# Weighted sums with V: from pT as the weights to V as the weights on four column tiles, with 32x32 transposes on VectorE

## The chip, the cores and the metric

The kernel runs on one core of a Trainium2 chip. The metric is the device time of one execution in microseconds; the time before is the median of three runs. The profile is one execution taken by the hardware profiler; its times count from the first instruction of its span.

## The reference

Two branches share the input x (2048 x 512, bf16) and are mixed by a gate per row. Branch A is attention with a compressive memory: 32 heads of 16, four segments of 512 rows, each causal in itself, plus what a running memory M (16 x 16 for each head) of the earlier segments gives. Branch B is a gated feed-forward of width 1792.

```python
g = sigmoid((x * gate_w).sum(-1, keepdims=True))
out = g * A(x) + (1 - g) * B(x)

# A, for each head and each of 4 segments of L = 512 rows
p = softmax(qs @ ks.T * scale + causal_mask)
a_dot = p @ vs
a_mem = (phi(qs) @ M) / (phi(qs) @ z + 1e-6)
o = sig(beta) * a_mem + (1 - sig(beta)) * a_dot
M += phi(ks).T @ vs ; z += phi(ks).sum(0)
# A = concat(o) @ wo ;  phi(t) = t + 1 if t > 0 else exp(t)

# B
B = (gelu(x @ w_gate) * (x @ w_up)) @ w_down
```

## The kernel before, in words

Everything stays on the chip. x is held transposed (xT), and the weights are loaded once. The work falls into four segments (s = 0 to 3), each with four head groups of eight heads (c = 0 to 3), and each head group is worked off in five *visits of the logits*, A to E: 80 visits in all, numbered here from 1 (visit 32 is segment 1, group 2, B; visit 57 is segment 2, group 3, B).

A visit (`group_qk`, lines 514 to 545) computes logits for four heads at once: four matmuls in row tiles of 32, one for each head, into one PSUM tile `lg` of four banks, of which there is only one. ScalarE exponentiates it in one instruction of 128 x 2048 into a tile `pT` (bf16, five buffers), and GpSimd zeroes the triangle above the diagonal. Logits are laid out with keys on partitions and queries along the free dimension, so `pT` is the transposed softmax numerator. A and B are the even heads (p = 0), C serves both, D and E the odd heads (p = 1); each visit takes one or two blocks of 128 keys.

The sums of values with weights (`pv`, lines 547 to 555) use a 128x128 block of `pT` as the stationary operand and 17 columns of V (16 values and a column of ones) as the moving one: 1280 matmuls of 17 columns over the kernel, into `od`, with queries on partitions. `finish` (557 to 566) takes the reciprocal of the 17th column, multiplies it by the gate of the head (`og`), and scales into `o2`. For segments 1 to 3 the memory's share `tm` (`mem_num`, 497 to 510) is added to `o2`. Then a transposing DMA on SyncE's queue (`tr_o`, line 570) turns `o2` into `oT`, which the output projection `aT` (line 417) reads as weights; the last head group is transposed by TensorE instead.

Between the visits TensorE is filled with *units* of other work, out of named streams: K projections (`kT`, whose result VectorE copies to `ktb` and masks into `KT`, lines 297 to 305), Q (`qT`), V (`vT`), gate and up projections of branch B (`gT`, `uT`), its down projection (`dT`, 14 matmuls a unit), the output projection (`aT`), the memory update (`MT`, line 441, which reads `pk` = phi(K) transposed by DMA from `phk`, line 312), the denominators of the memory (`zd`, line 480). A unit ends in VectorE's emptying of its PSUM bank; these units share three banks (pool `gen`).

The order is computed when the program is built, by a planner inside the kernel. It keeps a time for TensorE (`t_pe`), one for ScalarE (`t_act`) and the work that VectorE has not yet done (`backlog`), with a price for each step (`passed(pe, dve)`). In each visit it issues the logits, then what is due (`later(n, f)` puts a step n visits ahead), then fills TensorE up to a goal. Among streams it takes the one with the smallest due time plus a penalty for VectorE's work while `backlog` is high:

```python
st = min(hs, key=lambda x: x.q[0][5] + WEIGH * x.q[0][1] / x.q[0][0] *
         (backlog[0] - 0.8))
```

What a visit cannot do without is forced by `need` before its logits, such as the K of its head group. Each engine then runs its own list strictly in that order, and so does SyncE with the DMAs that it issues (`oT`, `pk`, the stores of `osb`).

Of the kernel before, what the change touches and what calls it, by code (L numbers as in the profile page):

```python
# [13 lines left out]
P = 128  # L14
# [20 lines left out]
EXP_T = 1.88  # L35
PHI_T = 1.06
# [8 lines left out]
def kernel(  # L45
# [54 lines left out]
    phk = const([P, NC8, L], BF, "phk")  # L100
# [5 lines left out]
    V = [const([P, KT, H, 18], BF, f"V{i}") for i in range(2)]  # L106
# [59 lines left out]
    def setup_consts():  # L166
        nc.gpsimd.memset(bm[:, :, :], 1.0)
        nc.gpsimd.affine_select(out=bm[:, :, :], in_=bm[:, :, :], pattern=[[-16, 8], [0, 17]],
                                compare_op=ALU.is_ge, fill=0.0, base=0, channel_multiplier=1)
        nc.gpsimd.affine_select(out=bm[:, :, :], in_=bm[:, :, :], pattern=[[16, 8], [0, 17]],  # L170
                                compare_op=ALU.is_ge, fill=0.0, base=15, channel_multiplier=-1)
        nc.vector.tensor_reduce(out=eo[:, 0:1], in_=bm[:, 0:8:2, 16],
                                axis=mybir.AxisListType.X, op=ALU.add)
        nc.vector.tensor_reduce(out=eo[:, 1:2], in_=bm[:, 1:8:2, 16],
                                axis=mybir.AxisListType.X, op=ALU.add)
        for i in range(2):
            nc.gpsimd.memset(V[i][:, :, :, 16:17], 1.0)
        nc.gpsimd.memset(Macc[:, :, :, :], 0.0)
# [8 lines left out]


# [76 lines left out]
    def phi(dst, src, key, lag):  # L265
        e = wk2.tile([P, 2, L], BF, name="phe", tag="phe")
        a = wk2.tile([P, 2, L], BF, name="pha", tag="pha", bufs=1)

        def f_exp():
            nc.scalar.activation(e[:, :, :], src, AF.Exp)  # L270
            act(PHI_T)

        def f_min():
            nc.vector.tensor_scalar(out=a[:, :, :], in0=src, scalar1=0.0, scalar2=1.0,  # L274
                                    op0=ALU.max, op1=ALU.add)
            nc.vector.tensor_tensor(out=dst, in0=e[:, :, :], in1=a[:, :, :], op=ALU.min)
            passed(0.0, 1.1)
            ready.add(key)

        later(lag, f_exp)  # L280
        later(lag + 1, f_min)
# [6 lines left out]
    def u_phk(s, c):  # L288
        def f():
            phi(phk[:, c:c + 2, :], ktb[:, c:c + 2, :], ("k", s, c), 1)  # L290
        return 0.0, 0.0, f
# [17 lines left out]
    def u_pk(s, c):  # L309
        def f():  # L310
            assert ("k", s, c - c % 2) in ready
            nc.sync.dma_start_transpose(pk[:, :, c * P:(c + 1) * P], phk[:, c, :])
        return 0.0, 0.0, f

    def u_v(s, kt):
        def f():
            T = gen("vT")
            for fc in range(FC):
                nc.tensor.matmul(T[:, :], lhsT=xT[:, fc, s * L + kt * P:s * L + (kt + 1) * P],  # L319
                                 rhs=wv[:, fc, :], start=(fc == 0), stop=(fc == FC - 1))  # L320
                if fc < FC - 1:
                    yield MM512
            nc.vector.tensor_copy(V[s % 2][:, kt, :, 0:16],
                                  T[:, :].rearrange("p (h d) -> p h d", h=H))
            return MM512
        return 4 * MM512, EVAC, f
# [107 lines left out]
    def u_M(s, half):  # L434
        def f():
            T = gen("MT")
            Tv = T[:, 0:272].rearrange("p (c h e) -> p c h e", c=2, h=8)
            for cc in range(2):
                c = 2 * half + cc
                for kt in range(KT):  # L440
                    nc.tensor.matmul(Tv[:, cc], lhsT=pk[:, kt, c * P:(c + 1) * P],  # L441
                                     rhs=V[s % 2][:, kt, 8 * c:8 * c + 8, 0:17],
# [54 lines left out]
    def mem_num(s, c):  # L497
# [12 lines left out]
        tms[c] = tm  # L510


# [34 lines left out]
    def pv(s, c, p, qqs, od, blocks):  # L547
        for qq in qqs:
            for j in range(4):
                for kt in range(qq + 1):  # L550
                    t, off = blocks[(p, kt)]
                    o = off + (qq - kt) * P
                    nc.tensor.matmul(od[:, qq, j, 0:17], lhsT=t[:, j, o:o + P],  # L553
                                     rhs=V[s % 2][:, kt, 8 * c + 2 * j + p, 0:17],
                                     start=(kt == 0), stop=(kt == qq))

    def finish(c, p, od, o2):
        rden = wk2.tile([P, KT, 4, 1], F32, name="rden", tag="rden")
        nc.vector.reciprocal(rden[:, :, :, :], od[:, :, :, 16:17])  # L559
        nc.vector.tensor_tensor(  # L560
            out=rden[:, :, :, 0], in0=rden[:, :, :, 0],
            in1=og[:, None, 8 * c + p:8 * c + 8:2].to_broadcast((P, KT, 4)), op=ALU.mult)
        nc.vector.tensor_tensor(  # L563
            out=o2[:, :, p, :], in0=od[:, :, :, 0:16].rearrange("p q j d -> p (q j) d"),
            in1=rden[:, :, :, :].rearrange("p q j o -> p (q j) o").to_broadcast((P, KT * 4, DH)),
            op=ALU.mult)

    def tr_o(c, o2, oT, by_dma):
        if by_dma:
            nc.sync.dma_start_transpose(  # L570
                oT[:, c, :].rearrange("p (q t) -> p q t", q=KT),
                o2[:, :, :, :].rearrange("p q r d -> p (q r d)"))
            return
        T = pgen.tile([P, 1024], BF, name="oTp", tag="gen")
        for qq in range(KT):
            nc.tensor.transpose(T[:, qq * P:(qq + 1) * P],
                                o2[:, 4 * qq:4 * qq + 4, :, :].rearrange("p j r d -> p (j r d)"),
                                ident[:, :])
        nc.vector.tensor_copy(oT[:, c, :], T[:, 0:512])


# [128 lines left out]
    for i in range(NK, NSEG * NC8):  # L710
# [3 lines left out]
                       (s == 0 or ("k", s - 1, c - c % 2) in ready)))  # L714
# [70 lines left out]
    def after(s, c, g, blk, oT, st):  # L785
        if g == "A":
            st["o2"] = wk2.tile([P, KT * 4, 2, DH], BF, name="o2", tag="o2")
        if g in "AD":
            st["od"] = pod.tile([P, KT, 4, 32], F32, name="od", tag="od")
        od, o2 = st["od"], st["o2"]  # L790
        p, qqs = {"A": (0, [0]), "B": (0, [1]), "C": (0, [2, 3]), "D": (1, [0]),
                  "E": (1, [1, 2, 3])}[g]
        pv(s, c, p, qqs, od, blk)
        passed(0.1 * sum(q + 1 for q in qqs))
        if g in "CE":
            finish(c, p, od, o2)
            passed(0.0, 0.85)
        if g == "B" and s > 0:
            room_for_bank()
            mem_num(s, c)  # L800
            passed(0.3, EVAC)
        if g == "E":
            if s > 0:
                nc.vector.tensor_tensor(
                    out=o2[:, :, :, :].rearrange("p q r d -> p (q r d)"),
                    in0=o2[:, :, :, :].rearrange("p q r d -> p (q r d)"),
                    in1=tms[c][:, :, :, :].rearrange("p q h d -> p (q h d)"), op=ALU.add)
                passed(0.0, 0.43)

            def tr():  # L810
                last = s == NSEG - 1 and c == NC8 - 1
                if last:
                    room_for_bank()
                tr_o(c, o2, oT, not last)
                done["tr", s] = count(("tr", s)) + 1
            later(2, tr)

    pending = []
    state = {}
    act_left[0] = 4 * NC8 * 5 * EXP_T + 3 * (GELU_T + 4 * PHI_T)  # L820
    for s in range(NSEG):
        oT = wk2.tile([P, FC, L], BF, name="oT", tag="oT")
        oTs[s] = oT
        for c in range(NC8):
            for g in "ABCDE":
                clock[0] += 1
                if g == "A":
                    need(("k", s), c + 1)
                    need(("q", s), c + 1)
                    need(("v", s), KT)  # L830
                t = group_qk(s, c, g)
                passed(QK_T)
                if g == "A":
                    mine = {(0, 0): (t, 0)}
# [13 lines left out]
                ready_at = t_act[0]  # L848
                for f in due.pop(clock[0], []):
                    f()  # L850
                n = 4 * NC8 * 5 - clock[0]
                pe_left = left() - TAIL_FILL - KT * 4 * MM512 + n * (QK_T + 0.55)
# [10 lines left out]
                pending.append(lambda a=(s, c, g, mine, oT, state): after(*a))  # L863
    fill_to(t_pe[0] + TAIL_FILL * 0.55)
    for f in pending:
# [13 lines left out]
    def phi_now(dst, src):  # L879
        e = wk2.tile([P, 2, L], BF, name="phe", tag="phe")  # L880
        a = wk2.tile([P, 2, L], BF, name="pha", tag="pha", bufs=1)
        nc.scalar.activation(e[:, :, :], src, AF.Exp)
        nc.vector.tensor_scalar(out=a[:, :, :], in0=src, scalar1=0.0, scalar2=1.0,
                                op0=ALU.max, op1=ALU.add)
        nc.vector.tensor_tensor(out=dst, in0=e[:, :, :], in1=a[:, :, :], op=ALU.min)
# [33 lines left out]
    def general():  # L919
# [3 lines left out]
        for s in range(NSEG):  # L923
# [17 lines left out]
            for c in range(NC8):  # L941
                o2 = wk2.tile([P, KT * 4, 2, DH], BF, name="o2", tag="o2")
                if s > 0:
                    mem_num(s, c)
                for p in range(2):
# [5 lines left out]
                    od = pod.tile([P, KT, 4, 32], F32, name="od", tag="od")  # L951
                    pv(s, c, p, range(KT), od, tiles)
                    finish(c, p, od, o2)
                if s > 0:
                    nc.vector.tensor_tensor(
                        out=o2[:, :, :, :].rearrange("p q r d -> p (q r d)"),
                        in0=o2[:, :, :, :].rearrange("p q r d -> p (q r d)"),
                        in1=tms[c][:, :, :, :].rearrange("p q h d -> p (q h d)"), op=ALU.add)
                tr_o(c, o2, oT, True)
# [9 lines left out]
            if s < NSEG - 1:  # L969
                for c in range(0, NC8, 2):  # L970
                    phi_now(phk[:, c:c + 2, :], ktb[:, c:c + 2, :])
# [39 lines left out]
```

## Time and profile before

| | us |
|---|---|
| median of the runs (3) | 291.42 (291.14 to 291.95) |
| span of the profiled execution | 289.4 |
| around the span, against the median | 2.0 |
| TensorE busy | 277.4 |
| VectorE busy | 215.5 |
| ScalarE busy | 200.7 |
| GpSimd busy | 82.7 |
| logits from the first to the last | 28.7 to 272.6 |

The profiled execution's own time is not listed apart from its span; it is taken as the span plus what lies between it and the median. In a row of the groups stand line, engine, operation, output and input, shapes and count; behind the bar the busy time, the mean duration in ns, and the idle time of the engine ahead of it with what ended most of it. A row of the timeline gives the start, the duration, and in brackets the idle time ahead. Durations include a part that overlaps the next instruction: matmuls of 512 columns last 0.38 and follow each other every 0.216.

### The profile page before, as it was taken

The numbers are of one execution on the slowest core, as the hardware profiler recorded it, in microseconds if no ns is written. First come the engines' busy times: TensorE is split into PE (matmuls) and PEld (weight loads), VectorE is DVE, ScalarE is ACT, GpSimd is POOL, SyncE is SP. The second block draws the span as 40 slices with busy tenths as digits, with TensorE's granted clock in tenths as the row PEclk, the third lists the DMA queues.
The fourth block names the chain that finished last, engine by engine and source line by source line (L and its number), as shares of the span: only waits on it lengthen the run. The fifth ranks groups of instructions, "written<-read, shape, count | busy, mean of one in ns | idle before, by whom it ended". The sixth has DMA issues, their size and how long they took to land.

```text
span 289.4 us, 6869 instructions
## 1 busy us (share of the span) xinstructions
PE 277.4 (96%) x2915; PEld 137.7 (48%) x2965; DVE 215.5 (74%) x422; ACT 200.7 (69%) x125; POOL 82.7 (29%) x140
## 2 busy tenths in 40 slices
PE   7999999999999999999999999999999999999994
PEld 3444454555444454555445444445454544444451
DVE  1897589768777869977878968988768567775545
ACT  3246977678898776776898785767658968677700
POOL 4000224334204424333410424242423033342410
PEclk9999999999999999999999999999999999999999
DMA  7989941110000100410000001032101001000102
GB/s 221 325 223 229 328 58 20 36 20 2 20 0 2 20 20 18 94 20 20 18 20 18 2 2 36 3 75 36 39 0 39 2 0 20 18 20 22 39 18 77
DMA packets 29441, 15.82 MB, mean 55 GB/s; under 512 B 21984, under 2 KB 28384, under 8 KB 29408
## 3 DMA queue, kind: packets, MB, share of 16 engines
q1 hardware_dynamic: 29408, 15.35, 21.1%
q8 instruction: 24, 0.39, 0.6%
q14 instruction: 9, 0.07, 0.1%
HBM read 8.14 MB, written 2.10 MB: 35 GB/s over the span
## 4 chain that ended last, share of the span: by engine, by line
PE 56%; DVE 3%; issue 1%; DVEq 0%
PE dT L400 14%; PE uT L384 10%; PE od L553 7%; PE gT L363 6%; PE lg L526 6%; PE aT L417 4%; PE kT L297 2%; PE vT L319 2%; PE qT L242 2%; PE mn L503 1%; PE MT L441 1%; DVE ktb L302 0%; DVE G L371 0%; DVE pha L274 0%; DVE o L563 0%
## 5 line engine op out<-in xcount | busy, mean ns | idle before, releaser
L532 ACT ACTIVATE pT<-lg 128x2048 bf16<-128x2048 f32 x80 | 150.1, 1876 | 57.0 <-PE lg L526 45.7
L543 POOL TENSOR_SCALAR_AFFINE_SELECT pT<-pT 128x512 bf16<-128x512 bf16 x128 | 79.5, 639 | 192.7 <-ACT pT L532 192.7
L384 PE MATMUL uT<-xT,wup 128*128 128x512 bf16 x208 | 59.5, 379 | 1.3 <-issue 0.6
L363 PE MATMUL gT<-xT,wga 128*128 128x512 bf16 x211 | 57.0, 379 | 1.0 <-DVE G L371 0.4
L400 PE MATMUL dT<-wdn,G 128*128 128x512 bf16 x212 | 53.2, 379 | 1.1 <-issue 0.3
L553 PEld LDWEIGHTS <-pT 128*128 128x128 bf16 x1280 | 43.6, 96 | 17.7 <-issue 0.4
L553 PE MATMUL od<-V,pT 128*128 128x17 bf16 x1280 | 43.9, 170 | 0.1
L390 DVE TENSOR_TENSOR G<-uT,G 128x512 bf16<-128x512 f32 x56 | 38.3, 685 | 7.2 <-PE uT L384 6.8
L371 DVE CAST G<-gT 128x512 bf16<-128x512 f32 x42 | 28.8, 685 | 8.0 <-PE gT L363 7.7
L526 PE MATMUL lg<-QT,KT 32*128 32x384 bf16 (+3 forms) x512 | 31.7, 301 | 1.6 <-issue 1.5
L363 PEld LDWEIGHTS <-wga 128*128 128x128 bf16 x224 | 19.7, 97 | 22.8 <-issue 5.5
L400 PEld LDWEIGHTS <-G 128*128 128x128 bf16 x224 | 19.5, 97 | 22.2 <-issue 3.9
L384 PEld LDWEIGHTS <-wup 128*128 128x128 bf16 x224 | 19.2, 97 | 20.8 <-issue 5.0
L405 DVE TENSOR_SCALAR tB<-dT,omg 128x512 bf16<-128x512 f32 x16 | 12.0, 750 | 19.9 <-PE dT L400 19.8
L526 PEld LDWEIGHTS <-KT 32*128 32x128 bf16 x512 | 8.9, 92 | 29.9 <-issue 29.5
L378 ACT ACTIVATE G<-G 128x3584 bf16<-128x3584 bf16 x6 | 18.8, 3182 | 0.0
L559 DVE RECIPROCAL rden<-od 128x16 f32<-128x16 f32 x32 | 8.2, 256 | 13.4 <-PE od L553 13.2
L297 PE MATMUL kT<-xT,wk 128*128 128x512 bf16 x63 | 16.8, 380 | 0.3 <-DVE xT L162 0.2
L417 PE MATMUL aT<-wo,oT 128*128 128x512 bf16 x63 | 16.4, 379 | 0.5 <-DVE G L371 0.5
L242 PE MATMUL qT<-xT,wq 128*128 128x512 bf16 x57 | 16.2, 379 | 0.5 <-DVE QT L247 0.2
L319 PE MATMUL vT<-wv,xT 128*128 128x512 bf16 x64 | 16.4, 380 | 0.0
L369 ACT ACTIVATE G<-gT 128x512 bf16<-128x512 f32 x14 | 8.4, 597 | 9.5 <-PE gT L363 9.5
(84 smaller groups left out, 224.7 us busy)
## 6 DMA issues: line engine op xcount, KB each, us to landing
wga<-in_B_w_gate_dram SPq DMA_DIRECT2D x1, 1792.0 KB, 12.6
wup<-in_B_w_up_dram SPq DMA_DIRECT2D x1, 1792.0 KB, 9.1
wdn<-in_B_w_down_dram SPq DMA_DIRECT2D x1, 1792.0 KB, 9.1
out_dram<-osb SPq DMA_DIRECT2D x12, 128.0 KB, 1.7
G<-in_A_x_dram SPq DMA_DIRECT2D x1, 512.0 KB, 4.1
wk<-in_A_wk_dram SPq DMA_DIRECT2D x1, 512.0 KB, 5.0
wq<-in_A_wq_dram SPq DMA_DIRECT2D x1, 512.0 KB, 6.7
wv<-in_A_wv_dram SPq DMA_DIRECT2D x1, 512.0 KB, 8.7
```

Of the source, the lines that this page charges most:

```text
L297: nc.tensor.matmul(T[:, :], lhsT=wk[:, fc, c * P:(c + 1) * P], rhs=xT[:, fc, s * L:(s + 1) * L], start=(fc == 0), stop=(fc == FC - 1))
L319: nc.tensor.matmul(T[:, :], lhsT=xT[:, fc, s * L + kt * P:s * L + (kt + 1) * P], rhs=wv[:, fc, :], start=(fc == 0), stop=(fc == FC - 1))
L363: nc.tensor.matmul(T[:, :], lhsT=wga[:, fc, hs * P:(hs + 1) * P], rhs=xT[:, fc, s * L:(s + 1) * L], start=(fc == 0), stop=(fc == FC - 1))
L371: nc.vector.tensor_copy(G[s % NG][:, hs, :], T[:, :])
L384: nc.tensor.matmul(T[:, :], lhsT=wup[:, fc, hs * P:(hs + 1) * P], rhs=xT[:, fc, s * L:(s + 1) * L], start=(fc == 0), stop=(fc == FC - 1))
L390: nc.vector.tensor_tensor(out=g, in0=T[:, :], in1=g, op=ALU.mult)
L400: nc.tensor.matmul(T[:, :], lhsT=G[s % NG][:, hs, qt * P:(qt + 1) * P], rhs=wdn[:, hs, :], start=(hs == 0), stop=(hs == HS - 1))
L417: nc.tensor.matmul(T[:, :], lhsT=oT[:, fc, qt * P:(qt + 1) * P], rhs=wo[:, fc, :], start=(fc == 0), stop=(fc == FC - 1))
L526: nc.tensor.matmul(lg[:, j, off:off + n], lhsT=KTm[pp][32 * j:32 * j + 32, (NC8 * s + c) % NK, kt * P:(kt + 1) * P], rhs=QT[32 * j:32 * j ...
L532: nc.scalar.activation(pT[:, :, :], lg[:, :, :], AF.Exp, scale=DH ** -0.5)
L543: nc.gpsimd.affine_select(out=v, in_=v, pattern=pat, compare_op=ALU.is_ge, fill=0.0, base=0, channel_multiplier=-1)
L553: nc.tensor.matmul(od[:, qq, j, 0:17], lhsT=t[:, j, o:o + P], rhs=V[s % 2][:, kt, 8 * c + 2 * j + p, 0:17], start=(kt == 0), stop=(kt == qq))
```

## The change

V becomes the stationary operand. For one parity of a head group, once all its blocks of `pT` are there, a *lump* of 16 matmuls runs directly behind the logits of a visit: for each of four key blocks and each of four heads, 32 columns of V (16 values, ones, and what follows) are the weights on one of four column tiles, and up to 512 columns of `pT` stream. The lump of the even heads stands in visit E, that of the odd heads in B of the next head group. The result `od` has values on partitions and queries along the free dimension. VectorE transposes it in 32x32 blocks out of PSUM into `oq` (fp32), one visit later takes the reciprocal and scales into `o2` (`norm`), and two visits after the second lump transposes 32x32 blocks back into `oT` (`back`). The memory's share `tm` is now transposed by a DMA on SyncE's queue into `mT` as soon as it is computed, and added at `oT` (`add_mem`), three visits after the second lump; the DMAs of `oT` and the transposes on TensorE are gone.

Beside that: phi is computed in place (no `pha`, no `phk`), so `pk` is transposed from `ktb`, and a K unit may start only when the `pk` transpose of its head group in the segment before has been issued; V gets 16 more columns of ones at its end; the numerator (`mem_num`) is issued in visit B from a list of its own; the planner's prices change (`PV_T = 0.65` for a lump, 0.69 for the transpose, 0.7 for `norm`, 0.6 for `back`).

```diff
-    def pv(s, c, p, qqs, od, blocks):
-        for qq in qqs:
+    def pv(s, c, p, blocks):
+        od = pod.tile([P, L], F32, name="od", tag="od")
+        for kt in range(KT):
+            t, off = blocks[(p, kt)]
+            n = L - kt * P
             for j in range(4):
-                for kt in range(qq + 1):
-                    t, off = blocks[(p, kt)]
-                    o = off + (qq - kt) * P
-                    nc.tensor.matmul(od[:, qq, j, 0:17], lhsT=t[:, j, o:o + P],
-                                     rhs=V[s % 2][:, kt, 8 * c + 2 * j + p, 0:17],
-                                     start=(kt == 0), stop=(kt == qq))
-    def finish(c, p, od, o2):
...
+                h = 8 * c + 2 * j + p
+                nc.tensor.matmul(od[32 * j:32 * j + 32, kt * P:L],
+                                 lhsT=V[s % 2][:, kt, 18 * h:18 * h + 32],
+                                 rhs=t[:, j, off:off + n],
+                                 start=(kt == 0), stop=(kt == KT - 1),
+                                 tile_position=(0, 32 * j))
+        oq = wk2.tile([P, 16, 32], F32, name="oq", tag="oq")
+        nc.vector.transpose(oq[:, :, :].rearrange("p b r -> p (b r)"), od[:, :])
+        return oq
+    def norm(c, p, oq, o2):
+        rden = wk2.tile([P, 16, 1], F32, name="rden", tag="rden")
+        nc.vector.reciprocal(rden[:, :, :], oq[:, :, 16:17])
+        nc.vector.scalar_tensor_tensor(
+            out=o2[:, :, p, :], in0=oq[:, :, 0:16], scalar=ogs[:, c, p:p + 1],
+            in1=rden[:, :, :].to_broadcast((P, 16, DH)), op0=ALU.mult, op1=ALU.mult)
+    def back(c, o2, oT):
+        nc.vector.transpose(oT[:, c, :], o2[:, :, :, :].rearrange("p b r d -> p (b r d)"))
+    def add_mem(c, oT):
+        nc.vector.tensor_tensor(out=oT[:, c, :], in0=oT[:, c, :], in1=tms[c][:, :], op=ALU.add)
     def mem_num(s, c):
...
-        tms[c] = tm
+        mT = wk2.tile([P, L], BF, name="mT", tag="mT")
+        nc.sync.dma_start_transpose(mT[:, :].rearrange("p (q t) -> p q t", q=KT),
+                                    tm[:, :, :, :].rearrange("p q h d -> p (q h d)"))
+        tms[c] = mT
     def u_phk(s, c):
-            phi(phk[:, c:c + 2, :], ktb[:, c:c + 2, :], ("k", s, c), 1)
+            phi(ktb[:, c:c + 2, :], ktb[:, c:c + 2, :], ("k", s, c), 1)
     def u_pk(s, c):
-            nc.sync.dma_start_transpose(pk[:, :, c * P:(c + 1) * P], phk[:, c, :])
+            nc.sync.dma_start_transpose(pk[:, :, c * P:(c + 1) * P], ktb[:, c, :])
...
-                       (s == 0 or ("k", s - 1, c - c % 2) in ready)))
+                       (s == 0 or count(("pk", s - 1)) > c)))
+    def lump(s, c, p, st, oT):
...
+        oq = pv(s, c, p, st["blk"])
+        passed(PV_T, EVAC)
...
+        later(1, f_norm)
+        if p == 1:
+            later(2, f_back)
+            if s > 0:
+                later(3, f_add)
...
+                if g == "B":
+                    for f in waiting:
+                        f()
+                    waiting.clear()
+                if g == "E":
+                    lump(s, c, 0, state, oT)
+                    waiting.append(lambda a=(s, c, 1, state, oT): lump(*a))
...
+                if g == "A" and s > 0:
+                    pending.append(lambda a=(s, c): numerator(*a))
```

## The prediction

> **What bounds the kernel now.** I read the page's busy times and chain first, then the groups, then the timeline around single visits of the logits, then the issues of SyncE.
>
> ```profile
> PE 277.4 (96%) x2915; PEld 137.7 (48%) x2965; DVE 215.5 (74%) x422; ACT 200.7 (69%) x125; POOL 82.7 (29%) x140
> ...
> PE 56%; DVE 3%; issue 1%; DVEq 0%
> ...
> L532 ACT ACTIVATE pT<-lg 128x2048 bf16<-128x2048 f32 x80 | 150.1, 1876 | 57.0 <-PE lg L526 45.7
> ...
> L553 PE MATMUL od<-V,pT 128*128 128x17 bf16 x1280 | 43.9, 170 | 0.1
> ```
>
> TensorE (PE) is busy nearly all the time and holds the chain. The exps of ScalarE stand idle 57 us beside them, 45.7 of it waiting for logits. Is that slack large? The timeline of two visits that follow closely says no:
>
> ```profile
> 252.06 0.40 PE L526 MATMUL lg<-QT,KT 32*128 32x384 bf16 x8
> ...
> 252.39 0.76 PEld L400 LDWEIGHTS <-G 128*128 128x128 bf16 x5 [0.21 <-issue]
> ...
> 252.59 1.88 ACT L532 ACTIVATE pT<-lg 128x2048 bf16<-128x2048 f32 x1 [0.58 <-PE lg L526]
> ...
> 254.54 0.12 PEld L526 LDWEIGHTS <-KT 32*128 32x128 bf16 x8 [0.42 <-issue]
> ...
> 255.05 1.88 ACT L532 ACTIVATE pT<-lg 128x2048 bf16<-128x2048 f32 x1 [0.58 <-PE lg L526]
> ```
>
> There is one logits tile, so logits wait for the exp before and the exp for the logits. Where TensorE arrives early a visit still takes 1.876 + 0.58 = 2.456 us: a floor under every visit. Logits cost TensorE 0.33 (252.06 to 252.39) plus 0.10 by which the matmul ahead is stretched at the change of tile shape; that gives 0.43.
>
> I added up what the order of instructions puts between each logits and the next: 0.216 per 512-column matmul, 0.0247 per od matmul (36 stand for 0.89 in the chain), 0.43 per logits. Visits 1 to 79 before come to 240.0 us; the trace has 243.9 from the first logits (28.7) to the last (272.6). So TensorE streams nearly without holes, and 77 of the 79 visits lie above the floor.
>
> **The change, part by part.**
>
> *Removed on TensorE.* 1280 od matmuls x 0.0247 = 31.6 us, and four transposes at the end (0.2).
>
> *Added on TensorE.* 32 lumps of 16 matmuls in four column tiles. If the tiles run together a lump is (512+384+256+128) columns x 0.216/512 = 0.54, and it makes one more change of shape (0.11, the excess of the logits' 0.33 over their 512 columns): 0.65, or 20.8 us in all. Do they run together? The warm-up has this shape:
>
> ```profile
> 4.01 0.62 PE L151 MATMUL warm<-G 128*32 128x256 bf16 x8
> ```
>
> ```profile
> 4.01 0.14 PEld L151 LDWEIGHTS <-G 128*32 128x32 bf16 x8 [0.84 <-issue]
> ```
>
> Eight 256-column matmuls, each lasting 0.41 there, took 0.62 together; in series at that clock they would need 1.7. All loads were through by 4.15.
>
> *What of 31.6 - 20.8 = 10.8 us is kept.* In the order of the changed kernel visits 1 to 79 sum to 229.1, but 48 of them hold only some 2.37 us and are stopped by the floor. With 2.456 for those the sum is 233.4, so the gain is 240.1 - 233.4 = **-6.7 us**. A cheaper lump would hardly add to it.
>
> *VectorE.* Per pair of lumps it loses two finishes (reciprocal 0.26, two products 0.32 and 0.43) and gains two transposes of od, two reciprocals, two products, one transpose back. No row has a transpose. The nearest are 128x512 from PSUM at 0.685 (0.60 from start to start when queued) and 128x512 bf16 at 0.425 or, reduced, 0.677. I take 0.60 for both kinds, the PSUM row being nearest; ends 0.35 and 1.2, the latter if four-byte elements go at half rate. VectorE then works about 1.3 us more per head group, 21 us in all, and comes to some 0.85 of TensorE's time in most stretches instead of 0.72. On average that is hidden. It is not where TensorE waits for one particular result, in three kinds of place.
>
> *First: pk behind the new mT on SyncE.* oT transposes leave the queue, twelve mT transposes enter it, issued as soon as the numerator exists. Issue is in order, and each waits for its data:
>
> ```profile
> 116.43 0.36 SPq L430 DMA_DIRECT2D out_dram<-osb  x1
> 116.88 5.33 SPq L312 DMA_TRANSPOSE pk<-phk  x4
> ```
>
> ```profile
> DMA to landing us min/median/max: 2.5/2.7/4.9
> ```
>
> A transpose holds SyncE 1.2 to 1.3 us and lands 2.5 after its issue. Before, pk's first piece landed near 119.4 and MT read it at 122.5: 3 us to spare. In the new order the four pk issues of segment 1 stand behind an mT whose tm is produced in visit 32, and MT follows in visit 33. From the logits of visit 32: lump done 0.98, handed over 1.2; VectorE then has transpose 0.60, reduction 0.59, phi 0.51 + 0.61, G 0.60, the three rdm steps 0.98, tm 0.69: 5.8. mT occupies SyncE to 7.0, pk lands at 9.5 and 10.8, MT is through at 11.0. Without waits TensorE would be there at lump 0.98, uT 0.86, zd and mn 0.42, gT 0.43, logits 0.43, gT 0.43, MT 0.5: 4.1. **+6.9 us**, with the next logits behind it and so ScalarE.
>
> In segment 2 MT's second half is in visit 58, right behind the first, and its pk stands behind an osb store. From the logits of visit 57: VectorE 1.2, transpose, G, tm 1.8, phi 1.1, norm 0.6, osb 0.75: 5.5; store issue 5.9, pk lands at 8.4 and 9.7, MT through at 10.0 instead of 4.3. **+5.7 us**. Segment 0 has seven visits between the two and pays nothing. Bounds for the two: 0 each if VectorE is far ahead, 8 each with slow transposes or the longest landing (4.9).
>
> *Second: K in the last moment.* The planner prices VectorE's new work and pushes the K units, dear on VectorE, back until they are forced. In visits 40, 50, 55, 60 and 75 kT stands with 4, 0, 0, 4 and 2 matmuls between it and the logits that need it. From its last column to those logits: result 0.17, ktb 0.73, KT 0.40, two hand-overs 0.2: 1.5. Less what stands between (0.86, 0, 0, 0.86, 0.43): **+5.3 us**. Bounds 2 and 9. These visits hold 3.8 us or more, so the floor does not cover it. Before, kT stood at least a visit ahead.
>
> *Third: single banks.* Behind transposes VectorE empties the three general banks late; before, such waits were 0.3 to 0.6 apiece (TensorE idle 0.49 at 114.16). Some four more: **+2** (0 to 4).
>
> *Other edits.* phi in place: same instructions, 0. ktb is now read by the pk transposes before K may overwrite it; K comes six visits later or more, 0 (1 if late). Adding tm at oT instead of o2: same 0.43. The tail gets transpose, norms, back and add (some 3.2 us) against 13 dT matmuls (2.8): **+0.5**.
>
> *Clock.* The steps of the first loads (1.75, 2.17, 2.60, 3.03) are 0.43, twice 0.216, until 5.76; 3.4 us behind the last matmul the granted clock falls:
>
> ```profile
> 286.00:289.00 3.00, 0.00 (x0) 0.00 (x0) 0.37 (x2) 0.00 (x0) 0.00 (x0) 1.00 0.29 98
> 289.00:289.40 0.40, 0.00 (x0) 0.00 (x0) 0.00 (x0) 0.00 (x0) 0.00 (x0) 0.58 0.00 0
> ```
>
> The two pk waits leave TensorE idle for 4 to 5 us in a piece. If the clock falls there, some 4.4 us run at half speed as at the start, a loss of 2.2 each. I count one: **+2.2** (0 to 4.4). The Trainium skill (TensorE: Matmul & The Clock Gate, Part 1) says that the gate halves the clock after an idle window of about 3.4 us which runs free of the kernel. By that rule either idle may or may not contain a whole window, which gives the same 0 to 4.4; the trace's one fall agrees with the 3.4.
>
> **Sum** against the profiled execution: 289.4 - 6.7 + 6.9 + 5.7 + 5.3 + 2 + 0.5 + 2.2 = 305.3. Its span lies 2.0 under the median of 291.42, so 307.
>
> **Rivals.**
>
> *The waits don't bite (faster).* If pk has landed when MT comes and K's chain is hidden, only floor, banks and tail count: 291.4 - 6.7 + 2.5 = 287. For it: the average load of VectorE leaves 15%. Against it: the issue order, and durations that the trace has. It decides where the two pk waits and the K waits together fall under 4 us. 0.10, and 0.02 that the parts cancel to within 0.3% (what a measurement can tell here).
>
> *Slow transposes.* At 1.2 each od transpose adds 0.6 ahead of the two pk places and the five K places (4.2) and more bank waits (3): 314. No row excludes it. 0.14.
>
> *Loads that do not overlap.* If a round's four loads wait for the round before, 0.1 each round (a load of that shape lasts 0.106), a lump is 0.95: visits B and E rise from 2.36 to 2.66, 0.2 over the floor, 32 x 0.2 = 6.4: 313. The warm-up's loads speak against it: the second four were through before the second four matmuls began. 0.08. The Trainium skill (same page, Part 3) says that loads overlap running matmuls only where the row group differs, which column tiles share; the warm-up's rows disagree.
>
> *Column tiles in series.* A lump of 2.1: 32 x 1.5 more, over 345. Warm-up against it: 0.01.
>
> **Numbers.** The forecast's own case, 300 to 312: 0.57; waits at half size, 293 to 300: 0.08. Faster 0.10, same 0.02, slower 0.88. The range 296 to 318 leaves out the fast case and the extremes. The Trainium skill (VectorE: DVE Perf Modes, The three transpose paths) gives 311 ns for 128x128 bf16; by that an estimate for 512 columns is 0.71, and the sum 1 us more.
>
> **What would show it.** In the trace after: lumps of 0.65; logits at 2.46 us in most visits; TensorE idle 4 to 6 us before MT in visits 33 and 58, released by a DMA; 0.5 to 1.5 us before the logits of visits 41, 51, 56, 61, 76, released by KT; VectorE near 237 busy. I am wrong if MT waits under 2 us in both places, or if the transposes run far from 0.6.

## The result, and the profile after

The changed kernel takes 306.34 us (median, 305.73 to 306.76) against 291.28: ratio 1.0497 (1.0461 to 1.0534). The forecast was 307, slower.

First the page of the changed kernel: busy times, the granted clock in 40 slices, the shares of the chain, and two rows of the groups.

```profile
PE 279.7 (92%) x2193; PEld 118.5 (39%) x2193; DVE 236.3 (78%) x441; ACT 200.6 (66%) x125; POOL 84.2 (28%) x142
PEclk9999999999999999669999999999789999999999
PE 77%; DVE 14%; DMA 3%; issue 2%; ACT 2%; SPq 1%; DVEq 0%; ACTq 0%
L539 ACT ACTIVATE pT<-lg 128x2048 bf16<-128x2048 f32 x80 | 150.1, 1876 | 72.8 <-PE lg L533 67.4
L567 DVE STREAM_TRANSPOSE oq<-od 128x512 f32<-128x512 f32 x32 | 22.9, 715 | 16.8 <-PE od L561 16.4
```

TensorE has 772 matmuls fewer (by its weight loads, 2193 instead of 2965; the page of before lacks 50 matmul records) and yet 2.3 us more of busy time, in part because two stretches ran at half clock: warm_mt below, whose clock stays up, has 282.5 us, of which 36 added matmuls of 0.216 make 7.8, so 5.0 us less than here. VectorE's share of the chain went from 3% to 14%. The exps wait 72.8 us instead of 57.0.

TensorE's waits in the whole run (total, times, longest):

```profile
PE MT L447 <- DMA pk<-ktb: 10.4, 4, 5.0
PE lg L533 <- DVE KT L310: 4.2, 5, 1.2
PE gT L369 <- DVE G L396: 2.3, 1, 2.3
```

Where they lie is seen when the time between the logits of chosen visits is compared (starts in the timeline, us). Visits 32 and 33 lie in the column "30 to 35", visits 57 and 58 in "55 to 60":

| kernel | 1 to 30 | 30 to 35 | 35 to 55 | 55 to 60 | 60 to 80 |
|---|---|---|---|---|---|
| before | 88.80 | 13.32 | 64.06 | 13.54 | 64.14 |
| after | 84.40 | 22.99 | 66.06 | 23.28 | 62.80 |

So the changed kernel is ahead by 4.4 us at visit 30, loses 9.7 at each of the two places and 2.0 between them, and wins 1.3 behind them. With 0.3 won before the first logits and a tail as long as before that is 15.3 us, the difference of the two spans (304.7 against 289.4).

Place 1, SyncE's queue and then TensorE:

```profile
124.24 1.20 SPq L517 DMA_TRANSPOSE mT<-tm  x1
125.53 5.14 SPq L318 DMA_TRANSPOSE pk<-ktb  x4
```

```profile
122.49 0.59 PE L369 MATMUL gT<-xT,wga 128*128 128x512 bf16 x2 [2.35 <-DVE G L396]
...
128.00 0.63 PE L447 MATMUL MT<-V,pk 128*128 128x136 bf16 x4 [4.05 <-DMA pk<-ktb]
129.32 0.63 PE L447 MATMUL MT<-V,pk 128*128 128x136 bf16 x4 [0.69 <-DMA pk<-ktb]
```

mT, whose tm VectorE made until 124.2, stood ahead of all four pk transposes. The first two, which this MT reads, were held by nothing else: VectorE had finished their phi at 91.99. The phi of the other two was done at 121.84. MT was through (the next unit could start) 12.1 us after the logits of visit 32 (11.0 in the forecast). Place 2, the same two views:

```profile
215.50 0.34 SPq L436 DMA_DIRECT2D out_dram<-osb  x1
215.88 2.50 SPq L318 DMA_TRANSPOSE pk<-ktb  x2
```

```profile
218.34 0.64 PE L447 MATMUL MT<-V,pk 128*128 128x136 bf16 x4 [5.02 <-DMA pk<-ktb]
219.66 0.63 PE L447 MATMUL MT<-V,pk 128*128 128x136 bf16 x4 [0.69 <-DMA pk<-ktb]
```

Here it was 10.7 us (10.0 in the forecast). Elsewhere the floor is plain to see, in ScalarE's timeline near the end: exps of 1.88 with 0.5 to 0.6 between them, one every 2.4 us.

```profile
281.18 1.88 ACT L539 ACTIVATE pT<-lg 128x2048 bf16<-128x2048 f32 x1 [0.58 <-PE lg L533]
283.62 1.88 ACT L539 ACTIVATE pT<-lg 128x2048 bf16<-128x2048 f32 x1 [0.56 <-PE lg L533]
285.99 1.88 ACT L539 ACTIVATE pT<-lg 128x2048 bf16<-128x2048 f32 x1 [0.49 <-PE lg L533]
```

### The profile page after: what moved, and what is told of

It reads as the page before. It is cut to its first block, busy times and chain, and to the rows that moved or that the text cites. A ratio compares the mean times of both kernels' runs of the same rounds, so it can differ in the third digit from the quotient of the medians.

```text
span 304.7 us, 5365 instructions
## 1 busy us (share of the span) xinstructions
PE 279.7 (92%) x2193; PEld 118.5 (39%) x2193; DVE 236.3 (78%) x441; ACT 200.6 (66%) x125; POOL 84.2 (28%) x142
## 4 chain that ended last, share of the span: by engine, by line
PE 77%; DVE 14%; DMA 3%; issue 2%; ACT 2%; SPq 1%; DVEq 0%; ACTq 0%
PE dT L406 15%; PE uT L390 14%; PE gT L369 14%; PE lg L533 9%; PE od L561 7%; PE vT L325 4%; PE aT L423 4%; PE qT L249 4%; PE kT L303 4%; DVE ktb L308 2%; DVE KT L310 2%; DMA pk<-ktb 2%; DVE G L396 1%; DMA G<-in_A_x_dram 1%; ACT pT L539 1%
## 5 line engine op out<-in xcount | busy, mean ns | idle before, releaser
L539 ACT ACTIVATE pT<-lg 128x2048 bf16<-128x2048 f32 x80 | 150.1, 1876 | 72.8 <-PE lg L533 67.4
L550 POOL TENSOR_SCALAR_AFFINE_SELECT pT<-pT 128x512 bf16<-128x512 bf16 x128 | 81.4, 654 | 206.6 <-ACT pT L539 206.6
L369 PE MATMUL gT<-xT,wga 128*128 128x512 bf16 x224 | 59.3, 389 | 2.4 <-DVE G L396 2.3
L390 PE MATMUL uT<-xT,wup 128*128 128x512 bf16 x224 | 61.0, 385 | 0.5 <-DVE G L377 0.4
L567 DVE STREAM_TRANSPOSE oq<-od 128x512 f32<-128x512 f32 x32 | 22.9, 715 | 16.8 <-PE od L561 16.4
L406 PEld LDWEIGHTS <-G 128*128 128x128 bf16 x224 | 20.7, 98 | 25.3 <-issue 3.1
L533 PEld LDWEIGHTS <-KT 32*128 32x128 bf16 x512 | 11.0, 92 | 37.6 <-issue 30.5
L561 PE MATMUL od<-pT,V 128*32 128x256 bf16 (+3 forms) x512 | 23.3, 302 | 0.0
L249 PE MATMUL qT<-xT,wq 128*128 128x512 bf16 x64 | 17.4, 391 | 0.3 <-DVE QT L254 0.2
L573 DVE SCALAR_TENSOR_TENSOR o<-oq,ogs,rden 128x256 bf16<-128x256 f32 x32 | 16.6, 518 | 1.1
L561 PEld LDWEIGHTS <-V 128*32 128x32 bf16 x512 | 10.7, 96 | 12.2 <-issue 6.3
```

Of the source, the lines that this page charges most:

```text
L249: nc.tensor.matmul(T[:, :], lhsT=wq[:, fc, c * P:(c + 1) * P], rhs=xT[:, fc, s * L:(s + 1) * L], start=(fc == 0), stop=(fc == FC - 1))
L369: nc.tensor.matmul(T[:, :], lhsT=wga[:, fc, hs * P:(hs + 1) * P], rhs=xT[:, fc, s * L:(s + 1) * L], start=(fc == 0), stop=(fc == FC - 1))
L390: nc.tensor.matmul(T[:, :], lhsT=wup[:, fc, hs * P:(hs + 1) * P], rhs=xT[:, fc, s * L:(s + 1) * L], start=(fc == 0), stop=(fc == FC - 1))
L406: nc.tensor.matmul(T[:, :], lhsT=G[s % NG][:, hs, qt * P:(qt + 1) * P], rhs=wdn[:, hs, :], start=(hs == 0), stop=(hs == HS - 1))
L533: nc.tensor.matmul(lg[:, j, off:off + n], lhsT=KTm[pp][32 * j:32 * j + 32, (NC8 * s + c) % NK, kt * P:(kt + 1) * P], rhs=QT[32 * j:32 * j ...
L539: nc.scalar.activation(pT[:, :, :], lg[:, :, :], AF.Exp, scale=DH ** -0.5)
```

## The experiments

The theory: the loss is made of late results at named places (pk at two, K at five), of the half clock that the long waits bring, and of a floor that keeps most of TensorE's saving from being seen. The main rival: VectorE, with 21 us more work, is too full as such, and TensorE waits for whatever comes next. All edits are to the changed kernel unless said. Ratios are against the kernel before, which took 291.27 to 291.33 beside them. The five columns are read from the one profiled execution of each; those of late_m and short_lumps took 298.66 and 289.58 us, 1.3 and 2.1 over their medians, and each holds a window at half clock in the column "30 to 35".

| kernel | median us | ratio (95%) | 1 to 30 | 30 to 35 | 35 to 55 | 55 to 60 | 60 to 80 |
|---|---|---|---|---|---|---|---|
| warm_mt | 301.91 | 1.0374 (1.0355 to 1.0392) | 84.40 | 20.34 | 66.05 | 21.40 | 62.80 |
| queue_order | 297.58 | 1.0223 (1.0204 to 1.0241) | 84.40 | 16.03 | 66.05 | 20.99 | 62.79 |
| late_m | 297.40 | 1.0204 (1.0171 to 1.0237) | 84.40 | 16.99 | 66.66 | 16.79 | 67.61 |
| early_k | 296.32 | 1.0176 (1.0159 to 1.0193) | 84.40 | 22.39 | 65.43 | 15.12 | 62.05 |
| late_m_early_k | 290.96 | 0.9996 (0.9978 to 1.0014) | 84.40 | 15.59 | 65.39 | 15.51 | 63.64 |
| unpriced | 294.53 | 1.0097 (1.0068 to 1.0126) | 89.36 | 13.76 | 67.84 | 13.21 | 62.82 |
| transpose_twice | 320.51 | 1.1017 (1.0986 to 1.1048) | 88.38 | 23.53 | 69.79 | 23.39 | 66.13 |
| short_lumps | 287.51 | 0.9869 (0.9853 to 0.9886) | 83.76 | 17.04 | 64.82 | 15.51 | 62.15 |
| half_transposes | 287.54 | 0.9873 (0.9851 to 0.9896) | 84.14 | 14.69 | 65.04 | 15.51 | 61.58 |
| add_on_gpsimd | 294.83 | 1.0129 (1.0084 to 1.0174) | 84.39 | 17.24 | 65.15 | 16.41 | 64.22 |
| tuned | 288.02 | 0.9885 (0.9869 to 0.9902) | 85.39 | 14.40 | 63.68 | 15.30 | 62.77 |
| tuned_on_vector | 287.61 | 0.9871 (0.9852 to 0.9891) | 88.21 | 12.91 | 63.95 | 12.66 | 63.24 |

**warm_mt: the price of the clock alone.**

```diff
             T = gen("MT")
+            for i in range({(1, 0): 16, (2, 1): 20}.get((s, half), 0) * (not general_now[0])):
+                nc.tensor.matmul(T[:, :], lhsT=wq[:, 0, 0:P], rhs=xT[:, 0, 0:L],
+                                 start=True, stop=True)
```

> Ahead of the two MT units that wait for pk (segment 1 first half, segment 2 second half) 16 and 20 matmuls of 512 columns run into MT's own bank; the real matmuls overwrite them. They fill 3.5 and 4.3 us of the 4.05 and 5.02 us of idle time; the waits stay. It prices the clock alone. Theory: the granted clock stays full and the two drops cost what the forecast bounded, 2.2 each: 302 to 304. Rival (behind the waits the exps and VectorE set the pace, so a slow TensorE costs nothing): 306 within 1 us, though the clock stays full.

4.4 us came of it. At place 1 the added matmuls fill the idle time, and MT starts where it did (127.96 against 128.00):

```profile
123.76 3.62 PE L444 MATMUL MT<-xT,wq 128*128 128x512 bf16 x16
127.96 0.42 PE L450 MATMUL MT<-V,pk 128*128 128x136 bf16 x4 [0.58 <-DMA pk<-ktb]
```

Four MT matmuls take 0.42 instead of 0.63, and the clock row has no slice under 9. The half clock cost 2.65 us at place 1 (22.99 to 20.34) and 1.88 at place 2: the upper end of the forecast's bound for both together, not the one drop that it counted. The rival that a slow TensorE would cost nothing there is out.

**queue_order: mT and osb one visit later in SyncE's queue.**

```diff
-        nc.sync.dma_start_transpose(mT[:, :].rearrange("p (q t) -> p q t", q=KT),
-                                    tm[:, :, :, :].rearrange("p q h d -> p (q h d)"))
+        send = lambda: nc.sync.dma_start_transpose(
+            mT[:, :].rearrange("p (q t) -> p q t", q=KT),
+            tm[:, :, :, :].rearrange("p q h d -> p (q h d)"))
...
+            later(1, send)
...
-            nc.sync.dma_start(out2[q0:q0 + P, :], osb)
+            send = lambda: nc.sync.dma_start(out2[q0:q0 + P, :], osb)
...
+                later(1, send)
```

> In the changed kernel the transposing DMA of mT and the stores of osb are issued one visit later than now, so that the pk transposes stand ahead of them in SyncE's queue; MT and K stay where they are. Theory (in both places pk waits in the queue for another DMA's data): in place 1 pk can be issued when phi is done (121.84) instead of behind mT (125.44), 3.6 us less; in place 2 at 214.12 instead of behind the store (215.84), 1.7 less; 5.3 in all, and 2.6 more from the clock if the first idle no longer lets it fall: 298 to 301. Rival (VectorE's lateness alone makes pk late; the queue does not matter): 305 to 307, the waits for pk as long as before.

8.8 us came of it, a little more than expected: 7.0 at place 1, where MT no longer waits at all and the clock stays up, and 2.3 at place 2, where waits of 3.3 and 0.9 us are left. Place 1 gave more than expected because the expectation took the wrong phi: the first two pk transposes were issued at 113.92 instead of 125.53, long before 121.84. So in place 1 the order of the queue was enough to make the wait; in place 2 it was the smaller part.

**late_m and early_k: time for pk, and time for K.** In late_m:

```diff
+            pk_at[s, c] = clock[0]
...
-        us += [unit(u_M(s, half), 20 * s + 11 + 2 * half) for half in range(2)]
+        us += [unit(u_M(s, half), 20 * s + 11 + 2 * half, None,
+                    lambda s=s, half=half: clock[0] >=
+                    min(pk_at[s, 2 * half + 1] + 4, 20 * s + 20))
+               for half in range(2)]
```

> Each MT unit may start four visits after the last pk transpose that it reads was issued, at the latest in visit 20(s+1); nothing else is edited. Theory (the waits for pk in visits 33 and 58 cost their idle time, 4.05 + 0.69 and 5.02 + 0.69 us, and the half-speed clock behind them): these 10.4 us and both stretches of half speed go; up to 4 us come back as waits for a single bank, since VectorE is still late in visits 32 and 58: 306.3 - 10.4 - 3 (clock) + 0 to 4 = 293 to 297, the clock full throughout. Rival (VectorE's load as such is the cause; TensorE waits for whatever stands next): the following units wait for their banks as long as MT did, 302 to 306, with idle time moved to uT and gT.

8.9 us came of it, 0.4 short of what was expected. Both places fell, by 6.0 and 6.5 us, and no wait for pk is left. But the last 20 visits lost 4.8: at visit 75 the forced K had to let a dT unit of 14 matmuls end first, and ScalarE stood idle for 5.40 us. The wait of gT in visit 32 remained (2.35 us) and in the profiled execution brought the clock down by itself for 3.4 us.

In early_k, ahead of the logits of every visit D:

```diff
+                i = NC8 * s + c + 1
+                if g == "D" and i < NSEG * NC8:
+                    need(("k", i // NC8), i % NC8 + 1)
```

> Each K unit is forced two visits earlier, in visit D of the head group before it. Theory: the waits of the logits for KT (4.2 us in visits 41, 51, 56, 61, 76) go; phi and pk of segment 2 come two visits earlier too, MT with them, so the two waits for pk stay within 2 us of what they are: 306.3 - 4.2 = 302, between 300 and 303. Rival (VectorE's load as such): the same 4 us appear as bank waits, 305 to 307.

10.0 us came of it instead of 3 to 6, and for a reason that the expectation denies: place 2 lost its wait (23.28 to 15.12). SyncE's queue and TensorE in visits 56 to 58:

```profile
205.31 2.50 SPq L318 DMA_TRANSPOSE pk<-ktb  x2
```

```profile
209.62 0.41 PE L447 MATMUL MT<-V,pk 128*128 128x136 bf16 x4
```

K of the last head group of segment 2 came two visits earlier, so phi did, so pk was issued 4.3 us ahead of MT and ahead of the store of osb. The wait for pk in place 2 thus goes when K alone comes earlier, the queue being as it was; queue_order took 2.3 us at the same place, so the two prices do not add up. In the other columns, where 3.0 us of waits for KT are gone, only 0.6 (35 to 55) and 0.8 (60 to 80) came back. That the waits of the logits would turn into bank waits, as the rival has it, is true in part: those of uT grew from 0.4 to 2.0 us.

Both edits together:

> Both edits, MT four visits behind pk and K two visits earlier. Theory: the gains add up: 306.3 - 10.4 - 4.2 - 3 + 0 to 4 = 289 to 293, about the kernel before. Rival (VectorE's load as such): not below 300.

290.96, level with the kernel before. 15.4 us of the changed kernel's time was thus a matter of when its units are issued: none of them is left out, and VectorE is as busy as in the changed kernel (235.4 against 236.3). The rival, not below 300, is out for these 15 us. The gains do not add up, though: 8.9 and 10.0 alone, 15.4 together, mainly since each frees place 2.

**unpriced: why K was late.** The three prices that the planner puts on VectorE's work behind a lump are set to nothing:

```diff
-        passed(PV_T, EVAC)
+        passed(PV_T)
...
-            passed(0.0, 0.7)
...
-            passed(0.0, 0.6)
```

> In the changed kernel the planner's price for VectorE's new work is set to nothing (0.69 for the transpose of a lump, 0.7 for norm, 0.6 for back); only the order of the units changes by it, no unit is added or left out. In the order that follows, K of visits 41, 51, 56, 61 and 76 stands in visits 33, 42, 49, 55 and 71, pk of segment 1 in visit 28 and MT in 33, pk of segment 2 in 52 and MT in 56 and 60. Theory (the pricing puts K off, and with K phi, pk and MT; TensorE waits for results that are late and not for VectorE's load): both MT places and the K places are free of waits: 290 to 295. Rival (VectorE's load itself is what costs; a planner that does not see it fills VectorE worse): single banks take over, 302 or more.

11.8 us came of it, and no wait for pk or KT is left among TensorE's waits; the longest are now those for single banks:

```profile
PE gT L369 <- DVE G L377: 1.9, 1, 1.9
PE uT L390 <- DVE G L396: 1.4, 1, 1.4
```

Both sides were right in part. The two places are as short as before the change (13.76 and 13.21), and the later phi of segments 1 and 2 is done at 112.33 and 190.53 instead of 121.84 and 214.12, so the pricing did put K, phi and pk off. But the visits up to 30 take 5.0 us longer, and TensorE stands idle 5.9 us in them instead of 0.7: a planner that does not see VectorE's work pays in waits, mostly for banks.

**short_lumps and half_transposes: what still binds at 290.96.** Both start from late_m_early_k.

```diff
-            n = L - kt * P
+            n = L - kt * P if kt == 0 or general_now[0] else 32
...
-                nc.tensor.matmul(od[32 * j:32 * j + 32, kt * P:L],
+                nc.tensor.matmul(od[32 * j:32 * j + 32, kt * P:kt * P + n],
```

> The version with MT four visits behind pk and K two visits earlier (290.96), with the sums cut short: of each lump the 12 matmuls of key blocks 1 to 3 stream 32 columns instead of 384, 256 and 128, so that these parts of the sums are left out; the count of instructions and all waits stay. A lump should fall from 0.65 to about 0.40, 8 us in all on TensorE. Theory (some 20 of the 32 visits with a lump last 2.38 to 2.46 us, the floor of exp and logits, and cannot be shorter): not more than 12 x 0.25 = 3 us: 288 to 291. Rival (TensorE, busy 95%, is what bounds): the whole 8 us: 282 to 284.

```diff
+        if p == 1 and not general_now[0]:
+            return oqs[0]
         oq = wk2.tile([P, 16, 32], F32, name="oq", tag="oq")
+        oqs[0] = oq
```

> The version with MT four visits behind pk and K two visits earlier (290.96), without the transposes of od for the odd heads: norm of the odd heads reads the even heads' oq, so that their part of the output is left out. VectorE has 16 x 0.64 = 10.2 us less, TensorE the same work. It stands beside the run with short lumps, where TensorE had 8 us less and 3.45 came of it. Theory (VectorE's load still bites there, at the 14.2 per 22.9 us that the doubled transposes cost): 10.2 x 0.62 = 6.3 less, 283 to 286. Rival (with the late results gone only TensorE and the floor bind): 289.5 to 291.

A lump fell from 0.66 to 0.40 (118.37 less 117.97 in visit 32), 8.3 us in all, and 3.45 came of it: a little over the theory's 3, far from the rival's 8. Where the rest went stands among TensorE's waits: logits now wait for the exp ahead of them in 21 visits, where in late_m_early_k none does.

```profile
PE lg L536 <- ACT pT L542: 5.7, 21, 0.5
```

The half of the transposes took 11.0 us off VectorE's busy time, and 3.42 came of it, between theory and rival. Four of the ten executions of late_m_early_k hold a window at half clock; against the other six (290.14 to 290.97) both gains are nearer 3. Neither engine is the bound alone. In late_m_early_k 45 of 79 visits last 2.48 us or less, in the kernel before 4. For TensorE the floor thus takes most of what is given; for VectorE this is argued and not shown, and no run made the exps shorter.

**transpose_twice: the price of more load on VectorE.**

```diff
-        nc.vector.transpose(oq[:, :, :].rearrange("p b r -> p (b r)"), od[:, :])
+        for again in range(2):
+            nc.vector.transpose(oq[:, :, :].rearrange("p b r -> p (b r)"), od[:, :])
```

> In the changed kernel VectorE transposes od into oq twice, the second over the first: 32 x 0.715 = 22.9 us more for VectorE, 0.64 each when queued. It prices the load on VectorE. Theory (the load hides beside TensorE and bites only ahead of the two MT places, the five K places and some single banks): by the forecast's price for slow transposes, 0.6 x 7 = 4.2 and banks 3, scaled by 0.7/0.6: 8.4, so 312 to 317. Rivals: hidden altogether, 306 to 308; VectorE is the bound throughout, 325 to 330.

14.2 us for 22.9 of work (20.6 of busy time: 256.9 after 236.3), more than the forecast's price and less than all of it. The named places hardly moved (30 to 35: +0.5; 55 to 60: +0.1). The rest of the visits lost 11: waits that were not there before or were shorter.

```profile
PE lg L533 <- DVE KT L310: 5.4, 5, 1.9
PE gT L369 <- DVE G L396: 3.2, 1, 3.2
PE uT L390 <- DVE G L377: 1.8, 2, 1.4
PE mn L509 <- DVE G L396: 1.4, 2, 1.1
...
PE zd L486 <- DVE pq L282: 1.3, 1, 1.3
PE qT L249 <- DVE G L396: 1.2, 1, 1.2
```

So the rival's mechanism is there once VectorE is fuller by another tenth. It is not what made the changed kernel 15 us slower, since late_m_early_k has the same load.

**add_on_gpsimd, tuned and tuned_on_vector: better versions.** In add_on_gpsimd one word changes in late_m_early_k (`nc.vector.tensor_tensor` in `add_mem` becomes `nc.gpsimd.tensor_tensor`).

> The same version (290.96) with the twelve additions of mT to oT on GpSimd instead of VectorE; the order of everything else is as it was. VectorE has 12 x 0.43 = 5.2 us less. Theory (VectorE's load counts at 0.6 us per us): 287 to 289.5. Rivals: nothing comes of it, 290 to 291.5; or GpSimd and VectorE slow each other where they run together, above 291.5.

It cost 3.9 us. The twelve additions last 1.21 us on GpSimd against 0.40 on VectorE, VectorE's busy time did not fall (236.8 after 235.4), and its operations between SBUF tiles grew meanwhile. The groups of the two kernels, late_m_early_k first:

```profile
L282 DVE TENSOR_TENSOR ktb<-phe,ktb 128x1024 bf16<-128x1024 bf16 x6 | 4.5, 744 | 0.2
```

```profile
L584 POOL TENSOR_TENSOR oT<-oT,mT 128x512 bf16<-128x512 bf16 x12 | 14.5, 1210 | 3.6 <-DVE oT L581 3.6
```

```profile
L282 DVE TENSOR_TENSOR ktb<-phe,ktb 128x1024 bf16<-128x1024 bf16 x6 | 5.3, 881 | 0.2
```

In the second kernel five of these six last 0.69 to 1.00 us, as all do in the first; the sixth, at 199.59 beside an addition, lasts 1.52. Evictions from PSUM did not grow (679 and 681 ns). The Trainium skill (GPSIMD Engine Reference, Specifications and Engine selection) says that GpSimd shares its SBUF interfaces with VectorE and is about twice as slow for elementwise work on two inputs; these rows agree with the first and show three times for the second. Part of the 3.9 us is a window at half clock, behind a bank wait of 2.8 us; the one execution of four with a full clock still took 293.92.

> The changed kernel with MT three visits behind pk, K one visit earlier (visit E), mT and the stores one visit later in the queue, the twelve additions of mT moved to GpSimd (12 x 0.43 = 5.2 us off VectorE), and other figures in the planner: WEIGH 6, TURN 0.13, PV_T 0.6, TAIL_FILL 3.5. Theory (with the late results out of the way VectorE's load and the floor of the exps are what is left): a few us below 290.96 and below the kernel before, 285 to 289. Rival (the floor alone is left): no better than 290 to 291.

> The version with MT four visits behind pk and K two visits earlier, every addition on VectorE, the queue as in the changed kernel, the planner's price for VectorE's work behind a lump at nothing, and three figures of the planner: WEIGH 4, PV_T 0.6, TAIL_FILL 4.5. Theory (GpSimd's additions brought nothing, and the order of the units is what the tuned version gained by): below the kernel before and no worse than the version with the additions on GpSimd (288.02), 285 to 288. Rival (the additions on GpSimd were needed, VectorE's load binds): 289 to 292.

Against late_m_early_k the second of them differs only in what the planner is told:

```diff
-PV_T = 0.65
+PV_T = 0.6
-TAIL_FILL = 5.5
+TAIL_FILL = 4.5
-WEIGH = 5.0
+WEIGH = 4
...
-        passed(PV_T, EVAC)
+        passed(PV_T, 0)
```

(and the prices 0.7 and 0.6 at nothing). 288.02 and 287.61 both beat the kernel before, by 1.2 and 1.3%, and the changed one by 6%. The second needs no addition on GpSimd, so its rival is out. Which of the planner's figures gave the gain was not taken apart. Both stretches with a pk place are shorter in it than in the kernel before (12.91 and 12.66).

## Why the prediction was right, and where its terms were off

**The lump and the floor: right.** A lump takes 0.66 us (209.75 to 210.41 in visit 57) for the 0.65 of the sum, so column tiles and their loads do overlap, and both rivals on that are out. By that the rule of the Trainium skill (TensorE: Matmul & The Clock Gate, Part 3), that loads overlap only where the row group differs, does not hold for this shape; whether the background weight buffer that the same part names is what lets them through, no run here shows. In the changed kernel 42 of 79 visits last 2.48 us or less, where 48 were put on the floor. The floor itself lies a little lower than 2.456: 28 of these visits are shorter, down to 2.37, with 0.49 to 0.58 us between the exps. Outside the two places the visits gained 3.7 us of the 6.7, with 3.0 us of waits for K in them, which the sum books apart. short_lumps shows the step itself: a cheaper lump adds less than half of what it saves.

**The two places: right in mechanism, their sum right by two errors.** At place 1 the chain ran as forecast and later: tm done 6.5 us behind the logits of visit 32 (5.8), the queue free at 7.8 (7.0), pk landed at 10.3 (9.5). From warm_mt to late_m_early_k the places fall by 4.75 and 5.89 us, close to the waits for pk in the trace (4.74 and 5.71). That is what the waits cost without the clock: 10.6, where the sum had 6.9 + 5.7 = 12.6. The clock was 4.5 for both drops, where one of 2.2 was counted; they lasted 10.24 and 6.83 us and not 4.4. Mis-sized by -2.0 and +2.3: that these two cancel is luck. That pk stood behind mT was the cause in place 1 (queue_order). In place 2 the store of osb was the smaller part, and the late K ahead of phi and pk the larger; the forecast had these as separate terms. One reading of the trace before was off: pk's first piece landed there 3.6 us after its issue at 116.88, so 2 us were to spare and not 3; no term hangs on it.

**K in the last moment: 4.2 us of waits for 5.3.** The five places are where they were named, with 0.3 to 1.2 us each. Taking the waits out gave back less than they last (1.4 for 3.0, in early_k). unpriced shows the reason given (the planner's prices push K back). What was missed is that K's lateness was also what made pk late in place 2.

**Single banks +2: 2.3** in one place (gT in visit 32), and it stays in every version that keeps that order. **Tail +0.5: 0.**

**Transposes 0.60: right.** They last 0.715 (from PSUM) and 0.702 (back), and the next instruction starts 0.63 behind them when queued (119.20 to 119.83). The estimate of 0.71 from the Trainium skill (VectorE: DVE Perf Modes, The three transpose paths) agrees with the durations.

**Price of VectorE's load: the forecast's weakest step.** The rival "slow transposes" put it all on the named places, 7 us for 0.6 us a transpose. transpose_twice has 14 for 0.7, and 0.6 of it at the two MT places. Likewise "the waits don't bite" would have been 287; with the waits gone it is 291. short_lumps and half_transposes say that the floor and VectorE's load share the rest; how they share it is not shown.

## What to carry to other kernels

When work moves from a busy engine to one with 15% to spare, look for the results that pass through the second engine and are awaited soon after (here K to phi to pk to MT), and for what stands ahead of them in a DMA queue; follow each chain to its start before pricing its links separately. In a program that plans its own order, a new price changes when other units are issued, and that can cost more than the work it stands for. Where two engines take turns at one buffer, time taken off either is cut off at the floor of their turn.

## What the runs showed of the hardware

The clock does not need an idle stretch of 3.4 us to fall. In all runs the changes of the granted clock lie on a grid of 3.413 us, and a window in which TensorE was busy for less than about half of it is followed by half speed. Windows of the changed kernel on its grid (length, then the busy times of PE, PEld, DVE, ACT and POOL with the count of instructions, then the granted clock, the DMA share and GB/s):

```profile
117.92:121.33 3.41, 2.22 (x40) 1.21 (x33) 3.38 (x6) 2.43 (x2) 1.33 (x3) 1.00 0.00 0
121.33:124.74 3.41, 1.46 (x12) 0.33 (x11) 3.24 (x8) 1.22 (x1) 1.00 (x1) 1.00 0.00 0
124.74:128.15 3.41, 0.15 (x2) 0.15 (x3) 1.31 (x4) 0.66 (x1) 1.22 (x2) 0.50 0.38 81
128.15:131.57 3.42, 2.73 (x13) 1.24 (x11) 0.44 (x1) 0.00 (x0) 0.00 (x0) 0.50 0.56 111
131.57:134.98 3.41, 3.41 (x12) 0.99 (x11) 2.00 (x3) 1.88 (x1) 0.35 (x1) 0.50 0.00 0
```

The window with 1.46 us of work, which holds the last 1.2 of the bank wait of 2.35 and the first 0.8 of the wait for pk, already brings the clock down. One with 2.73 does not bring it back; the next, full one does. In tuned lies the emptiest window that left the clock up:

```profile
215.15:218.56 3.41, 1.81 (x25) 0.93 (x24) 3.27 (x8) 3.38 (x3) 1.47 (x2) 1.00 0.00 0
218.56:221.97 3.41, 3.41 (x17) 1.56 (x16) 2.35 (x6) 3.41 (x2) 0.00 (x0) 1.00 0.28 77
```

Over the profiles of all fourteen kernels, at full speed every window with 1.54 us or less of work was followed by half speed and every one with 1.81 or more by full speed: the limit lies between 45 and 53% of a window. On the way back it lies higher: at half speed windows with 2.31 or less stayed there and those with 2.75 or more returned; of two between, 2.54 returned and 2.73 did not. The Trainium skill (TensorE: Matmul & The Clock Gate, Part 1) gives a free-running window of 3413 ns, which the grid confirms, and lets the clock fall after an idle window, where these rows show that a half-empty one is enough. A wait of 2.35 us is therefore free or costs a window at half speed, as it falls on the grid: in late_m_early_k the same wait (2.4) left 1.89 and 2.58 us of work in two windows, and the clock stayed up; in late_m it left 1.07 in one, and the clock fell. That holds from one execution to the next as well: two of late_m's four took 296.42 and 296.62 us at a mean granted clock of 1.000, the other two 298.18 and 298.66 at 0.994.
